# Query scores of pairs 8 to 31: turned on TensorE, or in blocks on VectorE and through DRAM

## The chip, the core and the metric

One core of a Trainium2 chip. The metric is the device time of one execution of the program, in microseconds. One core runs everything; its engines are TensorE (PE: matmuls, with PEld for the loading of weights), VectorE (DVE), ScalarE (ACT), GpSimd (POOL) and SyncE (SP), which here issues most of the DMAs.

## What is computed

A linear attention with exponential features, followed by a mixer block; batch 8, 8 heads, 576 tokens, head dimension 64, 128 features:

```
def phi(x):
    proj = einsum('bhsd,df->bhsf', x, w_phi)
    proj = proj - max(abs(proj), axis=-1, keepdims=True)
    return concatenate([exp(proj), exp(-proj)], axis=-1)
q_p, k_p = phi(q), phi(k)
kv = einsum('bhsf,bhsd->bhfd', k_p, v);  z = sum(k_p, axis=2)
x = einsum('bhsf,bhfd->bhsd', q_p, kv) / (einsum('bhsf,bhf->bhs', q_p, z) + 1e-06)
# x as [batch, 576, 512]:
u = x + (relu(x.T @ w_tok1) @ w_tok2).T        # token mix, 576 -> 256 -> 576
out = u + relu(u @ w_ch1) @ w_ch2              # channel mix, 512 -> 1536 -> 512
```

## The kernel before, in words

**Work.** Heads are taken in 32 pairs (four pairs to a batch); a pair's 2 x 64 rows fill the 128 partitions. From pair 8 on (`ROWS` = `PLAIN` = 8) an operand of a matmul is split into a high and a low part and the product is summed from three matmuls (`mm3`, line 84); pairs 0 to 7 use plain float32 matmuls and another order of the numerators (`row_numerators`, `flip`).

**Streams.** Five generators write the program: `keys()` (line 280), `queries()` (347), `token_stream()`, `load_weights()` and `channel_stream()`. `weave` (635) advances them in turns by the costs that they yield, over a share for each. A scheduler then orders the instructions of each engine with a simulated timeline; once all weights are loaded, the instructions of keys and queries have a higher priority than the rest. On the chip every engine runs its instructions in that fixed order, and a semaphore wait holds up what stands behind it.

**Keys.** For each pair `less_max` (218) projects a group of tokens (PE, `ppk`), adds the two halves of the product (`partk`, ACT, line 246; `pk`, DVE, 248), takes the largest absolute value (`mxk`, 253) and subtracts it (`pmk`, POOL, 255); ScalarE takes the exponentials `kp` (299) and PE accumulates `pkv` (324), which is copied to `kv` (341, 343). `kv` has one buffer, so a pair's `kv` is written when the numerators of the pair before are done.

**Queries.** Each pair has four pieces (k, j): k is the half of the tokens (320 or 256 of them), j the head. One step of `queries()` does, in this order: the numerators of the piece before last, the turn of the last piece, the scores of the next. Scores are `less_max` with tokens on partitions and features along them (`pmq`; the 64 last tokens of both heads are a tile of their own, `pmt`). `turn` (388 to 409) brings features to the partitions: PE transposes of 128x128 against an identity into PSUM (`pt`, line 393), three of them for k = 0 and two for k = 1, then four exponentials on ScalarE (`qf`, line 400, and rounded to float32r `qh`, 406, each with both signs), and the low parts `ql` (407, DVE and POOL). `qf`, `qh` and `ql` have two buffers each. `numerators` (463) runs `mm3` into `pn`, ScalarE copies to `xt` (478), VectorE turns the denominators in blocks (479, 484), and POOL multiplies `xt` (486).

**Buffers of a batch.** `xt0` (tokens of k = 0) has two buffers and `xt1` three: a batch's attention, its token mix (500) and the channel mix (549) of its tokens all work in them, and the channel mix's result is stored to `out_x` from there (607, 608). The channel mix goes in 18 chunks of 256 tokens (a batch has 2.25), each 6 times up (`h`) and down (`acc`). A chunk waits until the batches of its tokens are mixed, and a batch's `xt0` is free again when the chunks over its tokens are stored. PSUM: `pt`, `pn`, `ppq`, `ppt`, and from batch 1 on `pa`, `ph` and `px` share three banks (`REST`, line 56).

**Rows of batches 0 and 1.** `row_numerators` writes `rows` (438), five units of 128 tokens for a pair of pairs, two buffers; `flip` and the token mix (506) read it.

**SP's queue.** In one line: `raw` (266, one buffer, a pair's queries and the next pair's keys), `v` (290, 292), weights (139), `out_x` (608).

Of the kernel before, what the change touches and what calls it, by code (L numbers as in the profile page):

```python
# [32 lines left out]
LAST = 15  # L33
LAG = 0.02
SCRATCH = 1024
CH = 256

SEG = [(0, 320), (320, 256)]
# [7 lines left out]
def mixer_kernel(ctx, tc, qk, vm, vt, w_phi, w1, w2, wc1, wc2d, out):  # L46
    nc = tc.nc

    cst = ctx.enter_context(tc.tile_pool(name="cst", bufs=1))
    wk = ctx.enter_context(tc.tile_pool(name="wk", bufs=2))  # L50
    ps_w = ctx.enter_context(tc.tile_pool(name="ps_w", bufs=1, space=PSUM))
    ps_k = ctx.enter_context(tc.tile_pool(name="ps_k", bufs=1, space=PSUM))
    ps_h = ctx.enter_context(tc.tile_pool(name="ps_h", bufs=1, space=PSUM))
# [4 lines left out]
    def streamed(pool, shape, dtype, **kw):  # L58

        n = 1  # L60
        for k in shape[1:]:
            n *= k
        t = pool.tile([P, n + 32], dtype, **kw)[:, 16:16 + n]
        if len(shape) == 3:
            t = t.rearrange("p (a b) -> p a b", a=shape[1])
        return t
# [278 lines left out]
        kvs[i] = both  # L345

    def queries():
        turned, split_up, row_major = None, None, None
        pieces = [(i, k, j) for i in range(B * NP) for k in range(2) for j in range(2)] + [None] * 3
        for piece in pieces:  # L350
            if row_major:
                flip(*row_major)
                yield 0.2
            row_major = None
            if split_up:
                yield from until(lambda: split_up[0] in kvs)
                if split_up[0] < ROWS:
                    row_major = row_numerators(*split_up)
                else:
                    numerators(*split_up)  # L360
                yield 0.75
            split_up = None
            if turned:
                split_up = turn(*turned)
                yield 0.25
            turned = None
            if piece:
                i, k, j = piece
                if (k, j) == (0, 0):
                    plain = 0 if i < PLAIN else None  # L370
                    if i < PLAIN:
                        yield from until(lambda: i in pairs)
                        ts = pairs[i]
                    else:
                        yield from until(lambda: i + 1 in raws or i + 1 == B * NP)
                        if i + 1 == B * NP:
                            load(i + 1)
                        ts = stack(raws[i + 1], 0, f"q{i}")
                    asked.add(i)
                    tail = less_max(ts, [None], f"t{i}", plain, i < NP)  # L380
                    yield 0.11
                pm = less_max(ts, [(j, 2 * k), (j, 2 * k + 1)], f"q{i}_{k}{j}", plain, i < NP)
                turned = (i, k, j, pm, tail)
                yield 0.22

    def turn(i, k, j, pm, tail):
        w = SEG[k][1]
        ptr = ps_w.tile([P, 3, P], F32, **REST, name=f"pt{i}_{k}{j}")
        rows = [pm[:, 0], pm[:, 1]]
        if k == 0:  # L390
            rows.insert(2 * (1 - j), tail[:, 0])
        for n, r in enumerate(rows):
            nc.tensor.transpose(ptr[:, n], r, ident)  # L393

        o = D if k == 0 and j == 1 else 0
        src = ptr.rearrange("p u s -> p (u s)")[:, o:o + w]
        qps = []
        for sg in range(2):
            full = wk.tile([P, SEG[0][1]], F32, tag="qf", name=f"qf{i}_{k}{j}{sg}")[:, :w]
            nc.scalar.activation(full, src, AF.Exp, scale=1.0 - 2.0 * sg)  # L400
            if i < ROWS:
                qps.append(full)
                continue
            hi = streamed(wk, [P, SEG[0][1]], F32R, tag="qh", name=f"qh{i}_{k}{j}{sg}")[:, :w]
            lo = streamed(wk, [P, SEG[0][1]], F32R, tag="ql", name=f"ql{i}_{k}{j}{sg}")[:, :w]
            nc.scalar.activation(hi, src, AF.Exp, scale=1.0 - 2.0 * sg)  # L406
            (nc.gpsimd if sg else nc.vector).tensor_tensor(lo, full, hi.bitcast(F32), op=ALU.subtract)  # L407
            qps.append((hi, lo))
        return i, k, j, qps
# [8 lines left out]
    def row_numerators(i, k, j, qps):  # L418

        b, p = divmod(i, NP)
        h, p = divmod(p, 2)
        n = 3 - k
        if j == 0:
            sums[0] = ps_w.tile([P, 2, 3, D + 1], F32, **REST, name=f"pr{i}_{k}")
        pn = sums[0]
        at = (D if j == 1 else 0) if k == 0 else 0
        for u in range(n):
            w, c = (P, at + u * P) if u < 2 else (D, 0 if j == 1 else 2 * P)  # L430
            for sg in range(2):
                nc.tensor.matmul(pn[:w, j, u], qps[sg][:, c:c + w], kvs[i][:, sg, j],  # L432
                                 start=j == 0 and u == 0 and sg == 0, stop=j == 1 and u == n - 1 and sg == 1,
                                 skip_group_check=True)
        if j == 0:
            return None
        if (b, h) not in rows_of:
            rows_of[b, h] = wk.tile([P, 5, 2 * P], F32, tag="rows", name=f"rows{b}_{h}")
        x = rows_of[b, h][:, 3 * k:3 * k + n, p * P:p * P + P].rearrange("p u (j d) -> p j u d", j=2)
        den = column(wk, 8, tag="dn", name=f"dn{i}_{k}", bufs=4)  # L440
        if i < NP:
            gates.append(den[:, :1])
        for w, a, e in ((P, 0, 2), (D, 2, 3))[:2 - k]:
            d = den[:w, 2 * a:2 * e].rearrange("p (j u) -> p j u", j=2)
            nc.vector.tensor_scalar(d, pn[:w, :, a:e, D], 1e-6, None, op0=ALU.add)
            nc.vector.reciprocal(d, d)
            nc.vector.tensor_tensor(x[:w, :, a:e], pn[:w, :, a:e, :D],
                                    d.unsqueeze(3).to_broadcast([w, 2, e - a, D]), op=ALU.mult)
        return i, k

    def flip(i, k):
        b, p = divmod(i, NP)
        make_xts(b)
        x = rows_of[b, p // 2][:, 3 * k:3 * k + 3 - k, (p % 2) * P:(p % 2) * P + P]
        pf = ps_w.tile([P, SEG[0][1]], F32, **REST, name=f"pf{i}_{k}")[:, :SEG[k][1]]
        for u in range(3 - k):
            w = P if u < 2 else D
            nc.tensor.transpose(pf[:, u * P:u * P + w], x[:w, u], ident[:w, :w])
        nc.scalar.copy(xts[b][k][:, p], pf)
        if k == 1:  # L460
            attended.add(i)
# [28 lines left out]
    def until(cond):  # L490
        while not cond():
            yield None
# [7 lines left out]
    def token_mix(b, h, xt):  # L500
        pa = bank(b, [P, NT, 256], f"pa{b}_{h}", 0)
        for u, (s0, w, _) in enumerate(UNITS):
            k = 0 if s0 < SEG[1][0] else 1
            o = s0 - SEG[k][0]
            if (b, h) in rows_of:
                px = rows_of[b, h][:, u].rearrange("p (c d) -> p c d", c=2)
            else:
                px = bank(b, [P, 2, P], f"px{b}_{h}_{u}", 1)
                for c in range(2):
                    nc.tensor.transpose(px[:w, c], xt[k][:, 2 * h + c, o:o + w], ident)  # L510
            if w < P:

                xs = streamed(wk, [P, 2, P], F32R, tag="xh", name=f"xs{b}_{h}")
                nc.scalar.copy(xs[:w], px[:w])
                nc.vector.tensor_tensor(xs[w:], px[:w], xs[:w].bitcast(F32), op=ALU.subtract)  # L515
                x_all = xs.rearrange("p c d -> p (c d)")
                for t in range(NT):
                    ts = slice(t * P, (t + 1) * P)
                    for w1 in (w1_h, w1_l):
                        nc.tensor.matmul(pa[:, t], w1[:, u, ts], x_all, start=False, stop=False,  # L520
                                         skip_group_check=True)
                yield 0.6
                continue
            xh = streamed(wk, [P, 2, P], F32R, tag="xh", name=f"xh{b}_{h}_{u}")[:w]
            xl = streamed(wk, [P, 2, P], F32R, tag="xl", name=f"xl{b}_{h}_{u}")[:w]
            split(xh, xl, px[:w], nc.scalar, nc.gpsimd if (b, h) in rows_of else nc.vector)
            for t in range(NT):
                ts = slice(t * P, (t + 1) * P)
                mm3(pa[:, t], (w1_h[:w, u, ts], w1_l[:w, u, ts]),
                    (xh.rearrange("p c d -> p (c d)"), xl.rearrange("p c d -> p (c d)")),  # L530
                    u == 0 and t == 0, u == 4, group_ok=True)
            yield 0.8
# [165 lines left out]
```

## Time and profile before

| | |
|---|---|
| three runs | 1129.95, 1130.73, 1130.96 us; median 1130.73 |
| the profiled execution | 1130.58 us; its span, first to last instruction, 1128.8 us |
| granted TensorE clock | 0.999 of 2.4 GHz |
| PE, DVE, ACT, POOL busy | 98%, 59%, 48%, 45% of the span |
| instructions | 24388 |
| DMA | 54.39 MB in 66164 packets |

How to read it: a matmul's duration runs from its start to a modelled end, and matmuls overlap, so the sum of durations is more than the time that PE gives to them, and the distance of their ends is what one costs in a full stream. In the waits, "A <- B" is engine A standing idle until B's result came. The chain follows the end of the run back, at each step to what released the instruction. A piece's place in time can be told by its `qf` (ScalarE) and `xt` (GpSimd, line 486) instructions, a chunk's end by line 607.

### The profile page before, as it was taken

The page shows a single profiled execution, that of the slowest core. Times are in us where ns is not written, and L with a number is a line of the kernel's source. Part 1 is how long each engine was busy: PE and PEld are TensorE (multiplying, and loading weights), DVE is VectorE, ACT ScalarE, POOL GpSimd, SP SyncE. Part 2 cuts the span into 40 slices and gives each one's busy share as a digit, 9 for nine tenths or more (in the row PEclk, how much of TensorE's full clock was granted, in tenths as well). Part 3 has the DMA queues.
Part 4 walks back from the last instruction along what each step waited for, and adds up shares of the span by engine and source line. Part 5 has one row for each costly group of instructions (what it writes and reads, how often), then busy time and mean ns, then how long its engine had stood idle before and what let it go on. Part 6 is the DMA issues. An engine that isn't in the chain of part 4 may idle for free.

```text
span 1128.8 us, 24388 instructions
## 1 busy us (share of the span) xinstructions
PE 1109.2 (98%) x9280; PEld 1092.9 (97%) x9280; DVE 669.1 (59%) x1655; ACT 542.7 (48%) x1589; POOL 512.0 (45%) x675
## 2 busy tenths in 40 slices
PE   8999999999999999999999999999999999999998
PEld 7998999989999999989999999999999999999998
DVE  7889864476575756677465573664756675542111
ACT  5766543445464644556454463544645565441110
POOL 2334332465464744756364472644645474330110
PEclk9999999999999999999999999999999999999999
DMA  7545401111110111111011110111101110000000
GB/s 210 169 127 163 138 16 43 32 52 33 29 54 20 33 33 51 33 51 33 20 33 51 33 51 1 52 33 38 46 19 33 51 33 12 20 1 19 20 20 20
DMA packets 66164, 54.39 MB, mean 48 GB/s; under 512 B 44992, under 2 KB 56768, under 8 KB 66048
## 3 DMA queue, kind: packets, MB, share of 16 engines
q1 hardware_dynamic: 64528, 52.41, 15.9%
q8 instruction: 74, 1.21, 0.4%
q10 hardware_dynamic: 1520, 0.43, 0.2%
q14 instruction: 42, 0.34, 0.1%
HBM read 43.38 MB, written 9.44 MB: 47 GB/s over the span
## 4 chain that ended last, share of the span: by engine, by line
PE 87%; DVE 5%; POOL 3%; ACT 2%; DMA 2%; issue 1%; SPq 0%; POOLq 0%; ACTq 0%; DVEq 0%
PE acc L84 26%; PE h L84 26%; PE pkv L324 9%; PE pn L84 6%; PE ph L84 3%; PE pa L84 3%; PE pt L393 3%; PE pr L432 2%; PE ppk L239 2%; PE ppq L239 2%; PE px L510 1%; POOL stq L214 1%; PE ppq L243 1%; PE ppk L243 1%; DMA raw<-in_w 1%
## 5 line engine op out<-in xcount | busy, mean ns | idle before, releaser
L84 PE MATMUL acc<-gh,wc 128*128 128x256 f32 x1728 | 342.6, 283 | 0.2 <-ACT gh L576 0.2
L84 PEld LDWEIGHTS acc<-gh,wc 128*128 128x128 f32 x1728 | 275.6, 188 | 0.8 <-ACT gh L576 0.7
L84 PE MATMUL h<-uh,wc_h 128*128 128x256 f32 x864 | 245.5, 285 | 0.6 <-DVE gl L577 0.5
L84 PE MATMUL h<-uh,wc_l 128*128 128x256 f32 x864 | 244.4, 283 | 0.0
L84 PE MATMUL h<-ul,wc_h 128*128 128x256 f32 x864 | 243.6, 282 | 0.8 <-POOL ul L557 0.8
L84 PE MATMUL acc<-gl,wc 128*128 128x256 f32 x864 | 241.9, 282 | 0.0
L84 PEld LDWEIGHTS h<-uh,wc_h 128*128 128x128 f32 x864 | 162.5, 188 | 2.0 <-DVE gl L577 1.6
L84 PEld LDWEIGHTS h<-ul,wc_h 128*128 128x128 f32 x864 | 162.8, 188 | 1.2 <-POOL ul L557 1.1
L84 PEld LDWEIGHTS acc<-gl,wc 128*128 128x128 f32 x864 | 162.7, 188 | 0.0
L84 PEld LDWEIGHTS h<-uh,wc_l 128*128 128x128 f32 x864 | 162.5, 188 | 0.0
L324 PE MATMUL pkv<-v,kp 128*128 128x65 f32 (+2 forms) x1152 | 156.3, 270 | 0.6 <-ACT kv L333 0.2
L299 ACT ACTIVATE kp<-pmk 128x256 f32<-128x256 f32 (+1 forms) x320 | 109.6, 393 | 94.0 <-POOL pmk L255 76.7
L577 DVE SCALAR_TENSOR_TENSOR gl<-h,gh 128x512 fp32r<-128x512 f32 x108 | 74.4, 689 | 131.0 <-ACT gh L576 127.3
L407 POOL TENSOR_TENSOR ql<-qf,qh 128x320 fp32r<-128x320 f32 (+1 forms) x96 | 80.7, 840 | 152.7 <-ACT qh L406 146.7
L400 ACT ACTIVATE qf<-pt 128x320 f32<-128x320 f32 (+1 forms) x256 | 103.7, 417 | 94.4 <-PE pt L393 76.9
L324 PEld LDWEIGHTS pkv<-v,kp 128*128 128x128 f32 x1152 | 146.1, 191 | 2.3 <-ACT kp L299 1.2
L576 ACT ACTIVATE gh<-h 128x512 fp32r<-128x512 f32 x108 | 64.8, 600 | 131.6 <-PE h L84 130.3
L557 POOL TENSOR_TENSOR ul<-xt,uh 128x64 fp32r<-128x64 f32 (+3 forms) x120 | 60.5, 531 | 95.4 <-ACT uh L556 94.6
L84 PE MATMUL pn<-qh,kv 128*128 128x320 f32 (+1 forms) x384 | 101.0, 302 | 1.8 <-DVE xs L515 1.8
L255 POOL TENSOR_TENSOR pmk<-pk,mxk 128x256 f32<-128x256 f32 (+1 forms) x120 | 71.9, 599 | 43.7 <-DVE mxk L253 23.5
L255 POOL TENSOR_TENSOR pmq<-pq,mxq 128x256 f32<-128x256 f32 x96 | 61.6, 642 | 62.8 <-DVE mxq L253 57.6
L214 POOL TENSOR_TENSOR stq<-raw,stq 64x512 fp32r<-64x512 f32 (+1 forms) x48 | 69.7, 1452 | 37.9 <-DVE stq L213 35.3
(124 smaller groups left out, 2251.6 us busy)
## 6 DMA issues: line engine op xcount, KB each, us to landing
raw<-in_qk SPq DMA_DIRECT2D x23, 576.0 KB, 3.8
rawc<-in_wc SPq DMA_DIRECT2D x24, 512.0 KB, 4.1
v<-in_vm SPq DMA_DIRECT2D x31, 256.0 KB, 3.4
out_x<-xt SPq DMA_DIRECT2D x12, 256.0 KB, 2.2
out_x<-xt SPq DMA_DIRECT2D x16, 192.0 KB, 2.0
pair<-in_qk SPq DMA_DIRECT2D x16, 160.0 KB, 4.0
pair<-in_qk SPq DMA_DIRECT2D x16, 128.0 KB, 3.8
raw<-in_w SPq DMA_DIRECT2D x8, 256.0 KB, 5.9
```

What stands on the lines that cost most here:

```text
L84: nc.tensor.matmul(o, a, m, start=first and i == 0, stop=last and i == 2, skip_group_check=group_ok)
L214: nc.gpsimd.tensor_tensor(t[lo:lo + D], src, t[base:base + D].bitcast(F32), op=ALU.subtract)
L239: nc.tensor.matmul(ps[:, i].rearrange("p two f -> p (two f)"), t[:, c:c + P], wp2.rearrange("p two f -> p (two f)"), start=True, stop=True)
L255: eng.tensor_tensor(pm[:, :n], pr, mx[:, :n].unsqueeze(2).to_broadcast([P, n, F]), op=ALU.subtract)
L299: nc.scalar.activation(kp[:, :len(us), sg], pm[:, :len(us)], AF.Exp, scale=1.0 - 2.0 * sg)
L324: nc.tensor.matmul(o, kp[:, n, sg], v, start=g == 0 and n == 0 and sg == 0, stop=u is None, skip_group_check=True)
L393: nc.tensor.transpose(ptr[:, n], r, ident)
L400: nc.scalar.activation(full, src, AF.Exp, scale=1.0 - 2.0 * sg)
L407: (nc.gpsimd if sg else nc.vector).tensor_tensor(lo, full, hi.bitcast(F32), op=ALU.subtract)
L557: nc.gpsimd.tensor_tensor(l[:, d:d + n], t[:, c, o:o + n], h[:, d:d + n].bitcast(F32), op=ALU.subtract)
L576: nc.scalar.activation(gh, ph, AF.Relu)
L577: nc.vector.scalar_tensor_tensor(gl, ph, 0.0, gh.bitcast(F32), op0=ALU.max, op1=ALU.subtract)
```

## The change

From pair 8 on `turn` no longer transposes on PE. In the step of its scores, `across` (new) turns `pm` in 32x32 blocks on VectorE into `tq`; when both heads of a half are there, one DMA writes `tq` to a DRAM buffer and four DMAs, one for each block of 32 features, read it back as `qt`, so that the blocks come to their places; the inner run of the reads is 32 floats. The exponentials read `qt` in SBUF. The turn of a piece comes three steps later than before (`BEHIND` = 3), and before each exponential a one-column POOL copy from the latest scores into the exponential's own output makes it wait for these. At the end of the stream (no scores left) up to two pieces are turned at a step, without such copies. `tq` and `qt` use the buffers of `rows`, which becomes two tiles (three units and two), two buffers each. `TURNED` = 4 takes all four pairs of a batch.

```
+BEHIND = 3
+TURNED = 4
...
+    dram = ctx.enter_context(tc.tile_pool(name="dram", bufs=4, space=bass.MemoryType.DRAM))
...
     def queries():
-        turned, split_up, row_major = None, None, None
-        pieces = [(i, k, j) for i in range(B * NP) for k in range(2) for j in range(2)] + [None] * 3
-        for piece in pieces:
+        waiting, split_up, row_major, pm = [], [], [], None
+        pieces = [(i, k, j) for i in range(B * NP) for k in range(2) for j in range(2)]
+        n = 0
+        while n < len(pieces) or waiting or split_up or row_major:
...
+            for work in split_up:
+                yield from until(lambda: work[0] in kvs)
...
+                    numerators(*work)
                 yield 0.75
+            split_up = []
+            while waiting and len(split_up) < 2 and (waiting[0][0] <= n or n >= len(pieces)):
+                due, work = waiting.pop(0)
+                split_up.append(turn(*work, pm if via(work[0]) and n < len(pieces) else None))
+                yield 0.02 if via(work[0]) else 0.25
...
                 pm = less_max(ts, [(j, 2 * k), (j, 2 * k + 1)], f"q{i}_{k}{j}", plain, i < NP)
-                turned = (i, k, j, pm, tail)
+                if via(i):
+                    across(i, k, j, pm, tail)
+                waiting.append((n + 1 + BEHIND * via(i), (i, k, j, pm, tail)))
                 yield 0.22
+            n += 1
+    halves = {}
+    def via(i):
+        return i >= ROWS and i % NP < TURNED
+    def across(i, k, j, pm, tail):
+        n = 5 - k
+        if j == 0:
+            halves[0] = wk.tile([P, n, F], F32, tag=f"rows{k}", name=f"tq{i}_{k}")
+        t = halves[0]
+        at = 0 if j == 0 else n - 2
+        nc.vector.transpose(t[:, at:at + 2], pm)
+        if j == 0:
+            if k == 0:
+                nc.vector.transpose(t[:, 2], tail[:, 0])
+            return
+        d = dram.tile([P, n * F], F32, tag=f"half{k}", name=f"dq{i}_{k}")
+        nc.sync.dma_start(d, t.rearrange("p u f -> p (u f)"))
+        full = wk.tile([P, n, F], F32, tag=f"rows{k}", name=f"qt{i}_{k}")
+        d = d.rearrange("(a i) (u b s) -> b i u a s", a=4, b=4, s=32)
+        for b in range(4):
+            nc.sync.dma_start(full[32 * b:32 * b + 32].rearrange("p u (a s) -> p u a s", a=4), d[b])
+        halves[i, k] = full.rearrange("p u s -> p (u s)")
-    def turn(i, k, j, pm, tail):
+    def turn(i, k, j, pm, tail, behind):
         w = SEG[k][1]
-        ptr = ps_w.tile([P, 3, P], F32, **REST, name=f"pt{i}_{k}{j}")
...
+        if via(i):
+            src = halves[i, k][:, j * w:j * w + w]
+        else:
...
+            if behind is not None:
+                nc.gpsimd.tensor_copy(full[:, :1], behind[:, 0, :1])
             nc.scalar.activation(full, src, AF.Exp, scale=1.0 - 2.0 * sg)
...
+            if behind is not None:
+                nc.gpsimd.tensor_copy(hi[:, :1], behind[:, 0, :1])
             nc.scalar.activation(hi, src, AF.Exp, scale=1.0 - 2.0 * sg)
...
-            rows_of[b, h] = wk.tile([P, 5, 2 * P], F32, tag="rows", name=f"rows{b}_{h}")
+            rows_of[b, h] = [wk.tile([P, 3 - c, 2 * P], F32, tag=f"rows{c}", name=f"rows{b}_{h}{c}")
+                             for c in range(2)]
```

Lines 441, 454 and 506, which index `rows`, follow the new shape.

## Rows read from the trace of the kernel before

**Rows 1.** The page, part 1: busy time and share of the span by engine.
```profile
PE 1109.2 (98%) x9280; PEld 1092.9 (97%) x9280; DVE 669.1 (59%) x1655; ACT 542.7 (48%) x1589; POOL 512.0 (45%) x675
```

**Rows 2.** Busy time by stretch: stretch, us, then per engine busy (instructions), clock, DMA, GB/s.
```profile
222.00:1012.00 790.00, 780.62 (x6545) 773.97 (x6545) 486.46 (x1197) 408.85 (x1246) 427.69 (x558) 1.00 0.12 34
```

**Rows 3.** Waits (who, for whom: us in total, times, longest); the first two from 222 to 1012.
```profile
PE pt L393 <- POOL pmq L255: 2.1, 3, 0.8
...
POOL ql L407 <- ACT qh L406: 146.7, 50, 7.0
...
DVE stk L213 <- DMA raw<-in_qk: 8.8, 3, 4.3
```

**Rows 4.** The chain that ended last, by line, from 222 to 1012.
```profile
by line: PE acc L84 27.4%; PE h L84 26.7%; PE pkv L324 10.3%; PE pn L84 8.8%; PE pa L84 3.9%; PE ph L84 3.6%; PE pt L393 3.3%; PE ppk L239 2.7%; PE ppq L239 2.6%; PE px L510 1.5%; POOL stq L214 1.3%; issue 0.8%; POOL pmq L255 0.6%; POOL ul 
```

**Rows 5.** PE's timeline at 610 us: start, length (us), line, operation, count.
```profile
610.38 0.36 PE L84 MATMUL h<-uh,wc_h 128*128 128x256 f32 x1
610.59 0.38 PE L393 MATMUL pt<-ident,pmq 128*128 128x128 f32 x2
610.80 0.27 PE L393 MATMUL pt<-ident,pmt 128*128 128x128 f32 x1
610.83 0.36 PE L84 MATMUL pa<-xl,w_h 128*128 128x256 f32 x1
```

**Rows 6.** Groups by line and shape, whole span: count | busy us, mean ns | idle before.
```profile
L299 ACT ACTIVATE kp<-pmk 128x256 f32<-128x256 f32 x256 | 93.4, 415 | 63.6 <-POOL pmk L255 47.6 <-DVE pmk L255 8.3 <-PE pkv L324 3.5
...
L393 PE MATMUL pt<-ident,pmq 128*128 128x128 f32 x256 | 53.9, 275 | 2.5 <-POOL pmq L255 2.1 <-DVE dn L446 0.3
...
L400 ACT ACTIVATE qf<-pt 128x256 f32<-128x256 f32 x128 | 48.0, 386 | 47.3 <-PE pt L393 39.5 <-PE pr L432 7.6
...
L484 DVE STREAM_TRANSPOSE den<-few 128x256 f32<-128x256 f32 x24 | 10.6, 443 | 0.6
...
L146 POOL COPY bitsc<-dn 128x1 f32<-128x1 f32 x12 | 1.9, 186 | 1.9 <-DVE dn L446 1.8
```

**Rows 7.** Queue; DMA issues (count, KB each, us to landing); SP's issue of one (ns min/median/max).
```profile
q1 hardware_dynamic: 64528, 52.41, 15.9%
...
v<-in_vm SPq DMA_DIRECT2D x31, 256.0 KB, 3.4
...
out_x<-xt SPq DMA_DIRECT2D x12, 256.0 KB, 2.2
...
v<-in_vt SPq DMA_DIRECT2D x62, 16.0 KB, 2.1
...
L292 SPq DMA_DIRECT2D v<-in_vt x62: 469/585/1194, 14.4 to 918.5; - x62
```

**Rows 8.** ScalarE's timeline at the hand-over from pair 23 to 24.
```profile
747.90 0.37 ACT L478 COPY xt<-pn 64x256 f32<-64x256 f32 x1
...
754.53 0.43 ACT L400 ACTIVATE qf<-pt 128x320 f32<-128x320 f32 x1
...
780.53 0.65 ACT L478 COPY xt<-pn 64x320 f32<-64x320 f32 x2 [0.58 <-DMA out_x<-xt]
```

**Rows 9.** Pair 8's start (one tile's instructions; first and last start), then two timelines at 350 us.
```profile
L406 ACT ACTIVATE qh<-pt x192: 372/432/499, 222.1 to 1006.1; 128x320 fp32r<-128x320 f32 x96, 128x256 fp32r<-128x256 f32 x96
...
L514 ACT CAST xs<-rows x4: 397/404/406, 54.5 to 231.1; 64x256 fp32r<-64x256 f32 x4
...
345.11 0.74 POOL L486 TENSOR_TENSOR xt<-xt,den 128x256 f32<-128x256 f32 x1 [0.24 <-DVE den L484]
...
356.85 0.76 DVE L607 TENSOR_TENSOR xt<-acc,xt 128x256 f32<-128x256 f32 x2 [1.45 <-PE acc L84]
```

**Rows 10.** The end: timelines of GpSimd and VectorE, then the chain in order of time.
```profile
1011.86 0.74 POOL L486 TENSOR_TENSOR xt<-xt,den 128x256 f32<-128x256 f32 x1 [1.09 <-DVE den L484]
...
1015.93 0.76 DVE L607 TENSOR_TENSOR xt<-acc,xt 128x384 f32<-128x384 f32 x2 [0.54 <-PE acc L84]
...
1025.06 4.23 PE h L84 x36
```

More of the change, by code (lines that the diff above doesn't have):

```diff
@@ L347, in queries @@
     def queries():
-        turned, split_up, row_major = None, None, None
-        pieces = [(i, k, j) for i in range(B * NP) for k in range(2) for j in range(2)] + [None] * 3
-        for piece in pieces:
-            if row_major:
-                flip(*row_major)
-                yield 0.2
[L354 to L358, printed above, removed]
+        waiting, split_up, row_major, pm = [], [], [], None
+        pieces = [(i, k, j) for i in range(B * NP) for k in range(2) for j in range(2)]
+        n = 0
+        while n < len(pieces) or waiting or split_up or row_major:
+            for done in row_major:
+                flip(*done)
+                yield 0.2
+            row_major = []
+            for work in split_up:
+                yield from until(lambda: work[0] in kvs)
+                if work[0] < ROWS:
+                    row_major += [done for done in (row_numerators(*work),) if done]
                 else:
-                    numerators(*split_up)
+                    numerators(*work)
                 yield 0.75
[L362 to L368, printed above, removed]
+            split_up = []
[3 more added lines that the diff above has]
+                yield 0.02 if via(work[0]) else 0.25
+            if n < len(pieces):
+                i, k, j = pieces[n]
                 if (k, j) == (0, 0):
@@ L382, in queries @@
                 pm = less_max(ts, [(j, 2 * k), (j, 2 * k + 1)], f"q{i}_{k}{j}", plain, i < NP)
-                turned = (i, k, j, pm, tail)
+                if via(i):
+                    across(i, k, j, pm, tail)
+                waiting.append((n + 1 + BEHIND * via(i), (i, k, j, pm, tail)))
                 yield 0.22
-    def turn(i, k, j, pm, tail):
-        w = SEG[k][1]
-        ptr = ps_w.tile([P, 3, P], F32, **REST, name=f"pt{i}_{k}{j}")
[L389 to L396, printed above, removed]
+            n += 1
[21 more added lines that the diff above has]
+    def turn(i, k, j, pm, tail, behind):
+        w = SEG[k][1]
+        if via(i):
+            src = halves[i, k][:, j * w:j * w + w]
+        else:
+            ptr = ps_w.tile([P, 3, P], F32, **REST, name=f"pt{i}_{k}{j}")
+            rows = [pm[:, 0], pm[:, 1]]
+            if k == 0:
+                rows.insert(2 * (1 - j), tail[:, 0])
+            for n, r in enumerate(rows):
+                nc.tensor.transpose(ptr[:, n], r, ident)
+            o = D if k == 0 and j == 1 else 0
+            src = ptr.rearrange("p u s -> p (u s)")[:, o:o + w]
         qps = []
@@ L437, in row_numerators @@
         if (b, h) not in rows_of:
-            rows_of[b, h] = wk.tile([P, 5, 2 * P], F32, tag="rows", name=f"rows{b}_{h}")
-        x = rows_of[b, h][:, 3 * k:3 * k + n, p * P:p * P + P].rearrange("p u (j d) -> p j u d", j=2)
+            rows_of[b, h] = [wk.tile([P, 3 - c, 2 * P], F32, tag=f"rows{c}", name=f"rows{b}_{h}{c}")
+                             for c in range(2)]
+        x = rows_of[b, h][k][:, :, p * P:p * P + P].rearrange("p u (j d) -> p j u d", j=2)
         den = column(wk, 8, tag="dn", name=f"dn{i}_{k}", bufs=4)
@@ L453, in flip @@
         make_xts(b)
-        x = rows_of[b, p // 2][:, 3 * k:3 * k + 3 - k, (p % 2) * P:(p % 2) * P + P]
+        x = rows_of[b, p // 2][k][:, :, (p % 2) * P:(p % 2) * P + P]
         pf = ps_w.tile([P, SEG[0][1]], F32, **REST, name=f"pf{i}_{k}")[:, :SEG[k][1]]
@@ L505, in token_mix @@
             if (b, h) in rows_of:
-                px = rows_of[b, h][:, u].rearrange("p (c d) -> p c d", c=2)
+                px = rows_of[b, h][k][:, u - 3 * k].rearrange("p (c d) -> p c d", c=2)
             else:
```

## The prediction

> **What bounds the kernel now.** I read the page's engine totals first: PE is busy 98% of the span, no other engine over 59% [rows 1]. An average can hide stages, so next the busy time by stretch: I cut the span where the first exponential of pair 8 runs (222) and where the last numerators are divided (1012). In the middle stretch, the only one that the change touches, PE is busy 780.6 of 790 us, DVE 486, ACT 409, POOL 428, DMA 12%, and the granted clock is 1.00 [rows 2]. Then the waits: PE's longest that the change touches is 2.1 us in total over the stretch, for the very transposes that go [rows 3]. Last the chain of that stretch: 3.3% of it, 26.1 us, are the transposes `pt` of line 393 [rows 4]. So PE's instruction stream sets the time, and what counts is what an instruction keeps PE from doing next, which is not its duration: these transposes last 275 ns each [rows 6], but overlap.
>
> **Term 1, PE: the transposes go.** Pairs 8 to 31 have 3+3+2+2 transposes each: 24 x 10 = 240. In the timeline a matmul `h` starts at 610.38 and lasts 0.36, so ends at 610.74; three transposes and one `pa` matmul later the end is 610.83+0.36 = 611.19 [rows 5]. Of these 0.45 us a 256-column matmul takes 0.12 (the next `pa` starts 0.12 after); 0.33 remain, 0.111 us per transpose. 240 x 0.111 = 26.6 us; the chain's 26.1 us say the same. Nothing comes onto PE: **-26.6 us**.
> By the Trainium skill (TensorE: Matmul & The Clock Gate, PE-mode transpose) a transpose takes about 390 ns in isolation and about 275 in a kernel; an estimate from 390 would be 94 us and a time of 1043. The trace agrees with the 275 as a duration and disagrees with it as a price in a full stream.
>
> **Term 2, VectorE.** Per pair four block transposes of 128x256 and one of 128x128. A 128x256 one is in the trace at 443 ns [rows 6]; the small one is shorter, and I take it as long: 24 x 5 x 0.443 = 53 us at most. DVE goes from 486 to 539 us in a stretch that shrinks to some 764: 71%. It lies beside PE's channel matmuls, price 0; if that cover were gone, 0.44 us in the chain of each piece.
>
> **Term 3, GpSimd.** Each turned piece gets four one-column copies that hold its exponentials back until the latest score is there; pair 31 is turned in the flush, without them: 23 x 4 x 4 = 368. The trace has this copy at 186 ns [rows 6]: 68 us, POOL from 428 to 496 of 764, 65%. Behind a copy stand `pm` subtractions, splits and `ql`; for them wait the key exponentials, and PE's `pkv` for those. Price 0 beside PE, but this is the least certain engine (rival 3).
>
> **Term 4, ScalarE.** The 384 exponentials read SBUF instead of PSUM. A 128x256 one lasts 386 ns from PSUM (`qf`), 415 from SBUF (`kp`) [rows 6]: +0.03 x 384 = 11 us on ACT, 55%. Price 0; PE's `pn` would wait for it.
>
> **Term 5, transfers.** Each half pair issues one write (320 or 256 KB) and four reads, on SP: 48 x 5 = 240 DMAs. The reads move 128-byte runs, 2560 in the larger half; no row shows that size. Bounds: `v<-in_vm` lands 1024 runs of 256 B in 3.4 us, `v<-in_vt` 64 in 2.1 [rows 7], so 1.3 us for 960 more, 1.35 ns each: 2560 take 2.1 + 3.5 = 5.6 us. The other end is the mean packet of the whole queue: 15.9% of 16 engines x 1128.8 us over 64528 packets is 44.5 ns on one engine, 2560/16 of them 7.1 us, plus 2.1 [rows 7]. With 0.4 for the transpose, 0.6 to issue the write and 2.2 until it lands (as `out_x` of 256 KB), the trip is 8.8 to 12.4 us; I take 8.8, `v` being nearest in kind. A step of the query stream is 790/96 = 8.2 us, three are 24.7: the trip is home in time, price 0. SP itself: five issues of about 0.58 us [rows 7] make 2.9 us, and about 2.2 of waiting for the write, per half; behind it queue the loads `raw` and `v` and the stores of outputs. A load that comes 5 us late costs little: VectorE's `stk` waited for `raw` three times in all, 8.8 us [rows 3].
>
> **Term 6, the lag.** Numerators of a piece come three steps later. Where does that meet something? `xt0` has two buffers, so a batch's numerators wait for a chunk two batches back to be stored: the numerators stand still from 747.9 to 780.5, released by an output DMA, while the next pair's first exponentials (754.5) are long done [rows 8]. There the lag is free, for scores can run further ahead. It is not free in two places. At pair 8 no lead exists yet: its first exponential ran at 222.1, the rows buffers, which it now shares with batch 1 (the split of that tile in two costs nothing else), are read from until 231.1 [rows 9], and three steps put it up to 24.7 us later, once; chunk 3 ends at 356.9, 12 us after batch 2's numerators (345.1) [rows 9], about what the token mix needs. At the end the last trip (8.8) delays batch 7: its numerators end at 1011.9, chunk 14 at 1015.9, and the channel matmuls run unbroken from 1025 [rows 10]. Together 0 to 34 us. PE has in both places the work of pieces scored ahead, and [rows 8] is the nearest case (lag absorbed), so I take a fifth: **+6 us**. A gain is possible too: the three PSUM banks lose a user, and of the 9.4 us that PE idles in the stretch [rows 2] some may close: down to -6.
>
> **Sum.** The profiled execution took 1130.6 us (span 1128.8, 1.8 around it), the median of the three runs is 1130.7: no difference worth carrying. 1130.6 - 26.6 + 6 = **1110**; with -6 to +16 in place of +6, 1098 to 1120.
>
> **Rivals.**
> 1. *Attention, not PE, sets the pace.* Against: PE's 98.8% in the stretch. For: at batches 2 and 7 chunk and attention meet within 12 and 4 us [rows 9, 10], and the same lines show it at 3 and 6, four of the six, so a PE that is faster may only reach the hand-over earlier and wait. Then only two batches' share is kept, 26.6 x 2/6 = 8.9, and the end pays the trip of 8.8: 1130.6 - 8.9 + 8.8 = 1130.5, between 1122 and 1133.
> 2. *The trip outlasts three steps.* Then each of 48 halves is late by the excess; the gain is gone at 26.6/48 = 0.55 us of excess, a trip of 25.3 us. At 27 us it is 48 x 2.3 = 110 us: 1214. Against: 8.8 to 12.4 from the rows. It would take packets at about three times the dearer of the two prices, so the chance is small.
> The Trainium skill (DMA: Bandwidth & Descriptors, Specifications) asks for transfers of at least 512 B for line rate and has read-modify-write below that; by it the reads would come out nearer to this rival. No row of this trace shows runs of 128 B.
> 3. *Slower: GpSimd becomes what PE waits for.* POOL runs in order; two to four copies (0.37 to 0.74 us) stand ahead of a `pm` subtraction, and each waits for a `qf` or `qh` buffer that the matmuls of the piece before must free, so POOL now idles where ACT did. It decides from 26.6/92 = 0.29 us per piece that reaches PE. With 0.37: 92 x 0.37 = 34, and the lag's 6: 1144; with 0.74, 1178. For: POOL gains the most instructions (368 on 558 in the stretch [rows 2]), and already waits 146.7 us for `qh` [rows 3]. Against: PE's own waits for POOL in the stretch are the 2.1 us that go [rows 3].
> The Trainium skill (VectorE: DVE Perf Modes, Rules for kernel authors) says to turn a 128x128 tile on TensorE if PSUM will do; by it the change is a loss, as in rival 3. The trace, with PE full and DVE at 62% of the stretch, is against it.
>
> **How the numbers follow.** Forecast 0.70, rival 1 0.13, rival 2 0.05, rival 3 0.12. A measurement of this kernel tells about 0.2% from no change, 2.3 us: faster means under 1128.4. All of the forecast's case and half of rival 1 (0.06) lie there: 0.76. Rival 1 within 0.2%: 0.05. Rival 1's rest with rivals 2 and 3: 0.19. The range 1098 to 1136 reaches over rival 1 and leaves out rival 2 (0.05), most of rival 3 (0.10) and a little below.
>
> **What would show it.** Right: `pt` is left with 80 transposes (pairs 0 to 7); 120 VectorE transposes of about 0.44 us; 368 POOL copies of about 0.19; reads landing in 3 to 8 us; the stretch between pair 8's first numerators and the last about 20 us shorter at a PE busy share of still 98%; the end after the last numerators near 117 us as now. Wrong: PE idle of over 25 us in the stretch, with releasers `kp` or `pm` behind POOL copies (rival 3), `qf` behind a DMA (rival 2), or `uh`, `xh` at the hand-overs between attention and channel (rival 1). If the last numerators come no earlier than 1012, rival 1 was right.

## The result: 1137.5 us, slower by 0.6%

The median of four runs is 1137.51 us (1135.19 to 1140.06) against 1130.67: a ratio of 1.0058, 95% interval 1.0046 to 1.0070. The forecast was 1110 and the range ended at 1136; the change goes the other way.

### The profile page after: what moved, and what is told of

Same layout as the page of the kernel before. It is cut to its first block, busy times and chain, and to the rows that moved or that the text cites. A ratio compares the mean times of both kernels' runs of the same rounds, so it can differ in the third digit from the quotient of the medians.

```text
span 1134.9 us, 24670 instructions
## 1 busy us (share of the span) xinstructions
PE 1102.7 (97%) x9040; PEld 1082.1 (95%) x9040; DVE 717.6 (63%) x1775; ACT 565.7 (50%) x1589; POOL 568.2 (50%) x1043
## 4 chain that ended last, share of the span: by engine, by line
PE 77%; DVE 8%; POOL 6%; DMA 3%; ACT 3%; issue 2%; SPq 0%; ACTq 0%; POOLq 0%; DVEq 0%
PE h L87 23%; PE acc L87 23%; PE pkv L327 9%; PE pn L87 5%; PE ph L87 4%; PE pa L87 3%; PE pr L472 2%; DMA raw<-in_qk 2%; PE ppk L242 2%; PE ppq L242 1%; POOL stq L217 1%; PE px L551 1%; POOL stk L217 1%; PE ppk L246 1%; POOL pmq L258 1%
## 5 line engine op out<-in xcount | busy, mean ns | idle before, releaser
L87 PE MATMUL acc<-gh,wc 128*128 128x256 f32 x1728 | 337.1, 282 | 1.6 <-ACT gh L617 1.4
L327 PE MATMUL pkv<-v,kp 128*128 128x65 f32 (+2 forms) x1152 | 160.5, 274 | 5.4 <-DVE kv L346 4.7
L327 PEld LDWEIGHTS pkv<-v,kp 128*128 128x128 f32 x1152 | 151.5, 197 | 7.0 <-DVE kv L346 5.7
L87 PE MATMUL pn<-qh,kv 128*128 128x320 f32 (+1 forms) x384 | 105.8, 303 | 1.9 <-ACT qh L446 1.8
L438 ACT ACTIVATE qf<-qt 128x320 f32<-128x320 f32 (+1 forms) x192 | 83.3, 440 | 45.9 <-POOL qf L437 44.3
L446 ACT ACTIVATE qh<-qt 128x320 fp32r<-128x320 f32 (+1 forms) x192 | 83.5, 438 | 32.8 <-POOL qh L445 26.4
L217 POOL TENSOR_TENSOR stk<-raw,stk 64x512 fp32r<-64x512 f32 (+1 forms) x48 | 68.4, 1426 | 40.2 <-DVE stk L216 30.9
```

The lines of the kernel that those rows point to most:

```text
L87: nc.tensor.matmul(o, a, m, start=first and i == 0, stop=last and i == 2, skip_group_check=group_ok)
L217: nc.gpsimd.tensor_tensor(t[lo:lo + D], src, t[base:base + D].bitcast(F32), op=ALU.subtract)
L327: nc.tensor.matmul(o, kp[:, n, sg], v, start=g == 0 and n == 0 and sg == 0, stop=u is None, skip_group_check=True)
```

## The profile after

The page of the changed kernel, engines, slices and the DMA queue:

```profile
PE 1102.7 (97%) x9040; PEld 1082.1 (95%) x9040; DVE 717.6 (63%) x1775; ACT 565.7 (50%) x1589; POOL 568.2 (50%) x1043
...
PEclk9999999989997999999999899999999999999999
...
q1 hardware_dynamic: 185104, 80.74, 27.6%
```

The 240 transposes are gone (9280 to 9040 [rows 1]), yet PE's busy time fell by 6.5 us only, and its time outside busy grew from 19.6 us (span 1128.8 less 1109.2 [rows 1]) to 32.2 (1134.9 less 1102.7). The line of the granted clock, full in every slice before, has dips. The middle stretch, as in [rows 2]:

```profile
222.00:1012.00 790.00, 766.91 (x6236) 755.30 (x6236) 532.04 (x1307) 430.74 (x1240) 479.87 (x920) 0.98 0.28 70
```

So the profiled run (1136.7 us, 6.1 more than before's) is two losses against one gain: -26.6 for the transposes as forecast, +12.6 outside busy, and an estimate of +18.2 for the mean clock (0.999 less 0.983, times 1134.9 us); together +4.2.

**Single parts** came out as priced. Groups by line and shape, and the landing of the DMAs:

```profile
L407 DVE STREAM_TRANSPOSE tq<-pmq 128x256 f32<-128x256 f32 x96 | 42.0, 437 | 10.8 <-POOL pmq L258 10.0
L410 DVE STREAM_TRANSPOSE tq<-pmt 128x128 f32<-128x128 f32 x24 | 7.3, 305 | 3.3 <-POOL pmt L258 3.1
L445 POOL CAST qh<-pmq 128x1 fp32r<-128x1 f32 x184 | 36.7, 202 | 17.0 <-PE pn L87 15.1
L438 ACT ACTIVATE qf<-qt 128x256 f32<-128x256 f32 x96 | 38.8, 412 | 17.5 <-POOL qf L437 16.5 <-DMA qt<-dq 0.4
```

```profile
raw<-in_qk SPq DMA_DIRECT2D x23, 576.0 KB, 4.5
...
dq<-tq SPq DMA_DIRECT2D x24, 320.0 KB, 2.1
qt<-dq SPq DMA_DIRECT2D x96, 80.0 KB, 2.9
```

**Waits** that are new or longer (whole span; us, times, longest):

```profile
ACT kp L302 <- PE pkv L327: 70.0, 73, 4.4
...
ACT qf L438 <- POOL qf L437: 44.3, 63, 2.4
...
DVE stk L216 <- DMA raw<-in_qk: 25.5, 11, 4.1
...
PE pkv L327 <- DVE kv L346: 4.7, 2, 3.1
```

The key exponentials waited 3.5 us for `pkv` before [rows 6]. `kv` has one buffer and is written when the numerators of the pair before are done, so later numerators can hold up the keys. `raw` was 8.8 us in three waits [rows 3].

**Where the time goes.** Windows round the hand-over of batch 2 to chunk 4 (stretch, us, busy of PE, PEld, DVE, ACT, POOL, clock, DMA share, GB/s), then timelines in it:

```profile
340.00:350.00 10.00, 10.00 (x88) 10.00 (x87) 7.28 (x19) 6.29 (x20) 8.38 (x19) 1.00 0.28 69
350.00:360.00 10.00, 6.47 (x34) 4.72 (x33) 9.37 (x26) 5.56 (x17) 8.96 (x16) 0.86 0.48 120
360.00:370.00 10.00, 7.85 (x33) 6.45 (x31) 5.39 (x14) 4.17 (x11) 5.32 (x9) 0.50 0.44 114
```

```profile
350.29 0.76 DVE L648 TENSOR_TENSOR xt<-acc,xt 128x256 f32<-128x256 f32 x2 [0.27 <-PE acc L87]
...
365.32 0.41 PE L87 MATMUL pa<-xh,w_h 128*128 128x256 f32 x1
365.54 0.41 PE L87 MATMUL pa<-xl,w_h 128*128 128x256 f32 x1
...
369.68 0.71 POOL L527 TENSOR_TENSOR xt<-xt,den 128x256 f32<-128x256 f32 x1
...
381.63 0.28 PE L87 MATMUL ph<-w_h,ah 128*128 128x256 f32 x1
381.75 0.28 PE L87 MATMUL ph<-w_l,ah 128*128 128x256 f32 x1
```

Batch 2's last numerators come at 369.7 instead of 345.1 [rows 9]: 24.6 us, three steps, as the prediction had it. Chunk 3 ends at 350.3, 6.6 us earlier than before. The order is turned over: before, attention was done 12 us ahead of the chunk; now the channel mix has nothing to do for the 19 us until batch 2 is there. PE idles 3.5 of the ten us from 350, in gaps of 1.43 us at most; the clock falls to 0.50 (1.2 of 2.4 GHz), and 256-column matmuls start 0.22 us apart instead of 0.12.

The next such place is at 620 us:

```profile
617.78 0.62 SPq L269 DMA_DIRECT2D raw<-in_qk  x1
...
622.45 0.42 DVE L216 CAST stk<-raw 64x512 fp32r<-64x512 f32 x1 [2.95 <-DMA raw<-in_qk]
622.90 0.76 DVE L346 TENSOR_TENSOR kv<-pkv,kv 128x256 fp32r<-128x256 f32 x2
...
623.71 3.67 PE L327 MATMUL pkv<-v,kp 128*128 128x65 f32 x16 [3.09 <-DVE kv L346]
```

`raw` is issued between two reads of the trip, lands late, VectorE stands at `stk` for 2.95 us; behind `stk` in its order is the copy of `kv`, for which PE waits 3.09 us. In the stretch 620 to 630 the clock is 0.67.

## The experiments

The theories when they began, with the letters that the expectations use: the **lag** (A: late numerators starve the channel mix; later D: they also hold up `kv` and with it the keys), the **copies** (B: GpSimd, rival 3), and the **trip** (C: waiting for `qt`, or what its DMAs do to other loads). Times are medians; the ratio and its 95% interval are against the kernel before, run beside it.

### One part undone

**lag1**: `BEHIND` = 1.

```diff
-BEHIND = 3
+BEHIND = 1
```

> One number changed: the turn comes one step later than before the change, not three. Theory A (the lag of three steps delays batch 2's attention by 25 us, chunk 4 then starves, PE idles and its clock falls to half): two steps of 8.2 us less lag, so batch 2's last numerators about 16 us earlier than 369.7, the idle and half-clock time between 350 and 390 nearly gone, and 1137 - 15 = about 1122. Theory B (GpSimd's one-column copies delay pm and with it PE): as many copies, so 1133 to 1140. Theory C (SP's queue delays the loads raw): as many transfers, 1133 to 1140, or slower where the exponentials now wait for the trip.

1147.16 us, ratio 1.0146 (1.0129 to 1.0163). Batch 2 ends at 365.1, 4.6 us earlier and not 16, and the exponentials now wait for the trip:

```profile
ACT qf L438 <- DMA qt<-dq: 91.8, 40, 5.4
```

With a lag of three the same wait is 0.4 us in all. The lag does what it is for, and rival 2 falls.

**from12**: pairs 8 to 11 as before.

```diff
-        return i >= ROWS and i % NP < TURNED
+        return i >= 12 and i % NP < TURNED
```

> The change from pair 12 on; pairs 8 to 11 keep the transposes on TensorE and the old lag. Theory A: batch 2's attention ends near 345 as in the kernel before, chunk 4 starts on time, and at pair 12 the lag falls into the standstill for xt0; 200 transposes of 0.111 us go, 22 us, with the later losses of some 15 us kept: 1115 to 1125. Theory B or C: five sixths of the change's effect, so 1134 to 1137.

1137.42 us, 1.0060 (1.0045 to 1.0075): no difference, and the 1115 to 1125 of theory A is missed. Batch 2 ends at 344.7 as before, but the stall has moved one batch on (batch 3 ends at 495.3 instead of 476.9):

```profile
480.00:490.00 10.00, 6.35 (x20) 3.98 (x21) 7.70 (x21) 4.72 (x15) 9.56 (x17) 0.65 0.46 110
490.00:500.00 10.00, 8.84 (x40) 8.11 (x40) 3.94 (x11) 4.31 (x13) 4.03 (x7) 0.50 0.28 68
```

So the stall goes where the lag begins, and a lead over the channel mix did not absorb it.

**nogate**: no one-column copies.

```diff
-                split_up.append(turn(*work, pm if via(work[0]) and n < len(pieces) else None))
+                split_up.append(turn(*work, None))
```

> The change without the 368 one-column copies on GpSimd; the exponentials may go as soon as their qt has landed. Theory A: the order of the exponentials moves a little, the lag in the numerators stays, 1132 to 1140. Theory B: POOL falls from 568 to about 500 us busy, PE's idle time falls by 10 us or more, 1112 to 1125. Theory C: 1133 to 1140.

1135.55 us, 1.0040 (1.0025 to 1.0055): at best 2 us. `qf` then waits 64.1 us for `qt`, where it waited 0.4 with the copies. The keys wait far less:

```profile
ACT kp L302 <- PE pkv L327: 10.9, 12, 2.1
```

That wait falls from 70.0 us and the time hardly moves; but the wait for `qt` has come in its place, so this run prices neither.

**notrip**: no DMAs; the exponentials read `tq`, so the kernel leaves out putting the 32x32 blocks in their places; all sizes stay.

```diff
-        d = dram.tile([P, n * F], F32, tag=f"half{k}", name=f"dq{i}_{k}")
-        nc.sync.dma_start(d, t.rearrange("p u f -> p (u f)"))
...
-        halves[i, k] = full.rearrange("p u s -> p (u s)")
+        halves[i, k] = t.rearrange("p u s -> p (u s)")
```

> The change without the DRAM trip: the exponentials read the block-turned tile tq itself, so the 32 by 32 blocks stay where they are and the data is not put in place; the 240 transfers and SP's share in them are left out, VectorE's turns, the copies and the lag stay. Theory A: 1132 to 1140. Theory B: 1133 to 1140. Theory C: VectorE waits for raw 9 us as before the change instead of 25.5, PE's waits for kv behind it go, 1120 to 1130.

1124.35 us, 0.9942 (0.9927 to 0.9956). The trip costs 13 us, though in the change hardly anything waits for its end (0.4 us on ScalarE, 0.9 on GpSimd).

### Down to the floor

**notrip_lag1** is notrip with `BEHIND` = 1; **notrip_lag1_ng** also leaves the copies out; **notrip_ng** is notrip without the copies at lag 3.

> As notrip (exponentials read the block-turned tile, blocks not put in place, no transfers), and the turn comes one step later, not three. Theory D (kv has one buffer, so numerators that come three steps later hold up the keys, ScalarE's kp waits for pkv): those waits fall from 64 us in notrip to under 15, and the time from 1124 to between 1106 and 1115. If the lag has no price of its own: 1120 to 1128.

> As notrip_lag1, and without the one-column copies on GpSimd: what the change would give if the blocks came to their places at no cost. Theory B (the copies have a price): at least 5 us less than notrip_lag1. Otherwise within 3 us of it. A floor for the whole idea is 1131 - 26.6 = 1104.

> No transfers (blocks not put in place), lag of three steps, no one-column copies. If the copies make the lag (without them the scheduler lets the exponentials go early, and nothing holds the keys): 1103 to 1108, as with lag 1, and ScalarE's kp waits for pkv under 15 us. If the lag has its price without them: 1110 to 1120.

1112.31 (0.9844, 0.9827 to 0.9860), 1103.01 (0.9755, 0.9741 to 0.9770) and 1111.12 us (0.9824, 0.9810 to 0.9839). The page of notrip_lag1_ng, its wait of the keys, and the same wait in notrip_ng:

```profile
PE 1085.9 (99%) x9040; PEld 1070.1 (97%) x9040; DVE 715.9 (65%) x1775; ACT 559.0 (51%) x1589; POOL 509.8 (46%) x675
```

```profile
ACT kp L302 <- PE pkv L327: 3.5, 5, 1.4
...
ACT kp L302 <- PE pkv L327: 29.6, 36, 2.9
```

The turns, with exponentials from SBUF and a lag of one step, gain 27.7 us: terms 1, 2 and 4 together.

**idle_trip** is the other half alone: before's transposes and order of steps, with the VectorE turns and all 240 DMAs issued as work that nothing reads (`turn` always takes the PE branch, `BEHIND` out).

> The kernel before in its order of work (transposes on TensorE, no lag, no copies), with VectorE's block turns and all 240 transfers done beside it as work whose result nobody reads. Theory C (SP's queue and VectorE's load cost by themselves): 8 to 13 us more than before, 1139 to 1144, with VectorE waiting for raw some 20 us in place of 9. If they cost only where the exponentials wait for them: 1130 to 1134.

1132.97 us, 1.0017 (1.0008 to 1.0026): 2.2 us. The order on PE is not quite that of the kernel before: at 2279 of 9280 places another instruction stands.

**deadpe** keeps 240 PE transposes in the changed kernel, unread.

```diff
+                    idle = ps_w.tile([P, 3, P], F32, **REST, name=f"pd{i}_{k}{j}")
...
+                        nc.tensor.transpose(idle[:, m], r, ident)
```

> The change, and the 240 transposes on TensorE kept beside it as work whose result nobody reads (in the step of the scores). Theory A' (PE's own stream still sets the time, and the change only adds waits to it): 240 x 0.111 = 26.6 us come back, 1137 + 26.6 = 1160 to 1166. Theory D (attention with its lag sets the pace at the hand-overs, PE has time to spare there): most of the 26.6 us fit into the idle time and keep the clock up, 1137 to 1148.

1213.26 us, 1.0733 (1.0717 to 1.0749), outside both expectations. Inconclusive: the unread transposes take one of the three shared PSUM banks for a time, and wait there for `pm` (28.7 us), so it prices more than an instruction.

### What about the transfers costs 13 us

**dead_trip**: all DMAs, but the exponentials read `tq`; **dead_trip_lag1** the same with `BEHIND` = 1.

```diff
-        halves[i, k] = full.rearrange("p u s -> p (u s)")
+        halves[i, k] = t.rearrange("p u s -> p (u s)")
```

> Lag of three steps and the copies as in the change; all 240 transfers are issued and land, but the exponentials read the block-turned tile (blocks not put in place), so nobody waits for them. If the trip's 13 us come from the transfers' presence (SP's queue before raw, buffers held): 1133 to 1140, with VectorE waiting for raw over 20 us. If they come from the exponentials having to follow the trip: 1122 to 1128, notrip's 1124 plus the 2 us of idle_trip.

> The same with a lag of one step. If the 35 us between notrip_lag1 (1112) and lag1 (1147) are the exponentials' waits for the trip: 1111 to 1117. If the presence of the transfers costs as at lag 3: 1122 to 1128 or more.

1138.09 (1.0064, 1.0048 to 1.0079) and 1114.21 us (0.9848, 0.9832 to 0.9865). At lag 3 the presence of the transfers costs 13.7 us, at lag 1 only 1.9. These pairs are clean: on PE, VectorE, ScalarE and GpSimd, notrip and dead_trip hold the same instructions in the same order (4 of 9040 places differ on PE, 2 of 1775 on VectorE), and dead_trip has that of the change; at lag 1 no place differs. What differs can be followed at one place. Timelines of notrip, then of dead_trip, the same instructions:

```profile
358.24 1.53 POOL L217 TENSOR_TENSOR stk<-raw,stk 64x640 fp32r<-64x640 f32 x1
...
359.80 0.35 SPq L269 DMA_DIRECT2D raw<-in_qk  x1
...
363.29 0.42 DVE L216 CAST stk<-raw 64x512 fp32r<-64x512 f32 x1 [0.38 <-DMA raw<-in_qk]
```

```profile
361.30 1.53 POOL L217 TENSOR_TENSOR stk<-raw,stk 64x640 fp32r<-64x640 f32 x1
...
363.75 0.58 SPq L269 DMA_DIRECT2D raw<-in_qk  x1
364.38 2.35 SPq L417 DMA_DIRECT2D qt<-dq  x3
...
368.59 0.42 DVE L216 CAST stk<-raw 64x512 fp32r<-64x512 f32 x1 [2.63 <-DMA raw<-in_qk]
369.05 0.76 DVE L346 TENSOR_TENSOR kv<-pkv,kv 128x256 fp32r<-128x256 f32 x2
...
369.86 1.41 PE L327 MATMUL pkv<-v,kp 128*128 128x65 f32 x6 [2.50 <-DVE kv L346]
```

The buffer of `raw` is free when `stk` ends. Without transfers the load is issued 0.03 us later and lands in 3.5 us; with them 0.92 us later, behind a read, and it lands in 4.8. That is 2.2 us, which stand as 2.63 us of VectorE and then, because the copy of `kv` is queued behind, as 2.50 us of PE. Windows of two us, notrip and then dead_trip:

```profile
368.00:370.00 2.00, 2.00 (x19) 2.00 (x19) 0.55 (x2) 1.25 (x6) 0.00 (x1) 1.00 0.00 0
370.00:372.00 2.00, 2.00 (x18) 2.00 (x17) 1.60 (x6) 1.15 (x4) 0.49 (x2) 1.00 0.57 130
```

```profile
366.00:368.00 2.00, 1.35 (x8) 1.07 (x7) 0.00 (x0) 1.26 (x4) 0.00 (x0) 0.84 1.04 272
368.00:370.00 2.00, 0.14 (x1) 0.14 (x2) 1.35 (x4) 0.00 (x0) 0.85 (x1) 1.00 0.13 20
370.00:372.00 2.00, 2.00 (x11) 2.00 (x11) 1.52 (x5) 0.27 (x1) 1.92 (x3) 0.51 0.00 0
...
378.00:380.00 2.00, 2.00 (x10) 2.00 (x11) 0.48 (x2) 0.87 (x3) 0.00 (x0) 0.50 0.03 8
```

In notrip the clock is back at 1.00 from 364 on. In dead_trip it had just come back when PE was empty for nearly two us, and the next ten run at 0.50, with 11 matmuls in two us instead of 18. The sums say that this is nearly all: from notrip to dead_trip PE's busy time grows by 13.8 us for the same 9040 instructions, its time outside busy by 1.2.

As the order is one, each PE instruction of dead_trip can be set against the same one of notrip. By notrip's time it starts 0.3 us earlier at 223, 2.7 later at 243, 3.1 at 354, 10.1 at 375, still 10.1 at 597, 14.5 at 627 and 15.0 at the end. So three places make nearly all of it: 11 us fall where `raw` is late (the one above and one like that at 620), but the first 3 us do not. There the gaps of PE before the two rows below are as long in both (the longest 1.36 us), none of them for `raw`, and only the clock comes back later; why, no run shows. First notrip, then dead_trip:

```profile
238.00:240.00 2.00, 2.00 (x17) 2.00 (x17) 1.03 (x4) 0.78 (x3) 1.88 (x2) 1.00 0.00 0
```

```profile
238.00:240.00 2.00, 2.00 (x11) 2.00 (x11) 0.39 (x2) 0.34 (x2) 1.90 (x2) 0.50 0.60 95
```

The cells side by side (profiled runs; "outside" is span less PE busy):

| lag, copies, transfers | median us | PE busy | outside | clock |
|---|---|---|---|---|
| before | 1130.7 | 1109.2 | 19.6 | 0.999 |
| 1, no, none | 1103.0 | 1085.9 | 15.4 | 0.998 |
| 1, yes, none | 1112.3 | 1085.7 | 23.8 | 1.000 |
| 1, yes, unread | 1114.2 | 1088.5 | 24.2 | 0.998 |
| 3, no, none | 1111.1 | 1089.7 | 20.6 | 0.993 |
| 3, yes, none | 1124.4 | 1092.0 | 29.6 | 0.992 |
| 3, yes, unread | 1138.1 | 1105.8 | 30.8 | 0.978 |
| 3, yes, read (the change) | 1137.5 | 1102.7 | 32.2 | 0.983 |
| 3, no, read (nogate) | 1135.6 | 1100.2 | 34.4 | 0.989 |

Against the floor (the second row) the change has lost 33.6 us of span: 16.8 in PE's busy time for as many instructions, about what the lower clock accounts for (0.998 less 0.983, times 1134.9 us, is 17.0), and 16.8 outside it. What one part costs hangs on the others: without the copies the transfers cost 24.4 us at lag 3 (notrip_ng to nogate), with them 34.9 at lag 1 (notrip_lag1 to lag1), since in both the exponentials wait for `qt`.

### Other queues, lags and buffers

**raw_act** and **raw_pool** issue `raw` on ScalarE's and GpSimd's queue instead of SP's:

```diff
-                nc.sync.dma_start(raw[lo:hi], qk[i, lo:hi])
+                nc.gpsimd.dma_start(raw[lo:hi], qk[i, lo:hi])
```

> The change, with the 25 loads raw issued on ScalarE's queue, so that they no longer stand behind the trip's writes and reads on SP. Theory C (the trip's 13 us come from raw behind SP's queue): VectorE's waits for raw fall from 25.5 to about 10 us, the time from 1137 to 1124 to 1128. If the trip's price lies elsewhere (the order of work that the longer way of the scores gives): 1133 to 1140.

> The same with the loads raw on GpSimd's queue, which itself frees the buffer that they fill. Theory C: 1124 to 1130. Otherwise 1133 to 1142, as GpSimd also pays for issuing them.

1142.18 (1.0087, 1.0062 to 1.0112) and 1128.96 us (0.9978, 0.9961 to 0.9996); `stk` waits 14.2 and 17.0 us for `raw`, both less than 25.5. The control is **before_rawpool**, the kernel before with the same edit:

> Control: the kernel before, with the loads raw on GpSimd's queue. If raw_pool's 8 us came from the trip standing before raw in SP's queue: no gain here, 1129 to 1134. If those loads wait on SP in any case: 1121 to 1126.

1137.72 us, 1.0058 (1.0043 to 1.0073), with a clock of 0.998. The edit lets the scheduler write another order: at 2547 of 9280 places PE runs another instruction. `stk` also waits longer for `raw`, 17.3 us where it was 8.8 [rows 3], so queue and order are not told apart here. Either way the edit moves this kernel by 7 us where there is no trip to get out of the way of, and the +4.7 and -8.5 us of the two queues can't be put down to the trip standing before `raw`.

**lag2_ng** (`BEHIND` = 2, no copies), **rawpool_ng** (raw_pool, no copies) and **rawpool_lag2_ng** (both) look for a better point:

> The change with a lag of two steps and without the one-column copies: the lag and the copies cost less, the trip more, as exponentials may wait for it. If the two prices balance as between lag 1 (1147) and lag 3 (1137): 1134 to 1142. If the keys' hold-up weighs most: 1128 to 1133.

> The change with raw on GpSimd's queue and without the one-column copies. If the prices of SP's queue and of the copies add up: 1129 - 2 to 1129 - 9, so 1120 to 1127, faster than both kernels. If the exponentials then wait for the trip (64 us in nogate): 1127 to 1133.

> The same with a lag of two steps. If the exposed trip sets the time (lag2_ng 1143 against nogate 1136): 1130 to 1138. If the lag does: 1115 to 1125.

1143.47 (1.0111, 1.0096 to 1.0126), 1142.13 (1.0097, 1.0065 to 1.0130) and 1127.34 us (0.9968, 0.9951 to 0.9985). The last computes all of the reference and is faster than both kernels, by 0.3%, though its single runs lie between 1123 and 1132. raw_pool without its copies is 13 us slower; its exponentials then wait 51.4 us for `qt`, and `stk` 30.5 for `raw`. All three missed their expectations, so the parts did not add up as thought, and how much of that is the order's is not shown.

**psum2** gives `pkv` two PSUM banks and the shared users two instead of three:

> The change, with two PSUM banks for pkv and two instead of three shared by the rest (the transposes pt no longer use them from pair 8 on). Theory D (numerators three steps later hold the single kv, with it pkv and the keys): ScalarE's waits of kp for pkv fall from 70 to under 25 us, 1137 - 12 = about 1125, less what the lost bank costs. If the lag's price is another one: 1135 or more.

1215.18 us, 1.0745 (1.0729 to 1.0761), but the wait that the second bank was to end is gone, from 70.0 us:

```profile
ACT kp L302 <- PE pkv L327: 1.3, 2, 0.9
```

So the third shared bank is worth more than what `pkv` could gain, and the gain can't be read from this run. A second buffer for `kv`, with all banks left, was not tried.

## Why the prediction was wrong, step by step

- **Term 1** (-26.6) held: -27.7 down to the floor, and 23.3 of that in PE's busy time (1109.2 to 1085.9). The floor has another order than the kernel before, so a match within 1 us is closer than this can be known. The 0.12 us that it takes for a matmul is the distance of two ends, not of two starts as it says: the `pa` after the one at 610.83 starts at 611.03 and ends at 611.31, 0.12 after.
- **Terms 2 and 4** (price 0) held: 437 and 305 ns for a turn, 412 for an exponential from SBUF, and the floor, which holds both, is 1 us below what term 1 alone gives.
- **Term 6** (+6) failed: "[rows 8] is the nearest case (lag absorbed), so I take a fifth". The delay of 24.6 us and its place were right. But with the delay attention is 19 us behind the chunk there, and from12 shows that the lag is not absorbed where it begins later either. Without transfers two more steps of it cost 8.1 us without copies and 12.0 with them (1103.0 to 1111.1, 1112.3 to 1124.4). The step left out that PE, faster now, finishes chunk 3 earlier (350.3) while attention comes later, and that `kv` is held longer: without copies and transfers `kp` waits for `pkv` 29.6 us at lag 3 where it waits 3.5 at lag 1. Which of the two makes the price is not shown.
- **Term 3** (0) failed in its price, not in its duration (202 ns against 186). Without transfers the copies cost 9.3 us (lag 1) and 13.2 (lag 3), in the change 2.0. Copies and lag each come with another order (48 to 58% of PE's 9040 places differ), so these sizes hold whatever the order alone moves, which no run prices. Rival 3's 34 us and more is not there: no wait of PE for POOL is over 1.6 us in total.
- **Term 5** was right on the trip itself. In the change a write is issued at 349.64, and its four reads between 352.42 and 355.10; the last lands at 357.6. That is 8.0 us, with the turn's 0.4 8.4, against the 8.8 that was taken. It failed at "a load that comes 5 us late costs little", which took the three waits of [rows 3] as the price. What is queued behind `stk` on VectorE was not named: the copy of `kv`, and PE's `pkv` behind that. Price at lag 3: 13.7 us, shown by the pair in one order, of which the places with a late `raw` make 11 of 15 us in the profiled runs; at lag 1, where the clock stays at 0.998, 1.9.
- **The clock** is in no term. With 1.00 in the stretch before [rows 2] I took it as given; in the change PE idles 3.5 of ten us from 350 and 3.09 us in one gap at 620, the rows there show 0.50 and 0.67, and about half of what was lost against the floor is this. The Trainium skill (TensorE: Matmul & The Clock Gate, HAM oscillation — how this bites in real kernels) describes a kernel whose clock falls again at each wait of its matmuls for a DMA; the window from 368 in dead_trip, with 0.51 in the next, agrees.
- **The sum.** By one way up the table: 1103.01, lag +8.11, copies +13.23, transfers +13.74, reading what they bring -0.58: 1137.51. Another way gives other shares, as the cells show. Three costs that I had looked at one by one and each set at nothing or nearly so, because [rows 2] showed room on every engine.
- **Rivals.** The first came nearest: its sign, "the last numerators come no earlier than 1012", is met (1015.3), and the place is the hand-over between attention and channel. The other sign is not: PE idles 23.1 us in the stretch, under the 25 named, and its longest waits are for `kv` (4.7) and `gl` (4.1), not for `uh` or `xh`. Its price was too low, as it let PE wait at full clock and charged nothing for the load of `raw`. The second is refuted (0.4 us of waiting in all). The Trainium skill (DMA: Bandwidth & Descriptors, Specifications) asks for 512 B or more; the reads of 128-byte runs landed in 2.9 us, so the rule decided nothing here. The third is told under term 3.

Not settled: how much of the 8 to 13 us of lag and copies belongs to them and how much to the order that comes with them, why the clock came back later at 238 in dead_trip, and what a second buffer of `kv` would give back.

## What to carry to other kernels

Before a step is moved later, write down at every hand-over which side is ahead and by how much; where the lead is less than the delay, the consumer starves. When a DMA is put ahead of another in a queue, follow the waiting instruction to what stands behind it on its engine, down to the bottleneck. A gap of the busiest engine costs more than its length when the clock falls after it, so count gaps of TensorE at the clock that the rows show behind them, and where a scheduler writes the order, price an edit only against a pair with the same order or a control.

## What the runs showed that was not expected

- Two programs with one order and nearly equal idle time of PE (29.6 and 30.8 us) differ by 13.7 us, nearly all of it in PE's busy time, at a granted clock of 0.992 and 0.978.
- The nine runs of raw_act, one program, lie between 1132.8 us at a clock of 0.992 and 1145.8 at 0.976: once PE has gaps, its time is spread as well as longer. The kernel before, at 0.998 to 1.000, stayed within 1130.0 and 1133.3 beside it.
- An edit without a gain of its own, another queue for one load, slowed the kernel before by 0.58%, with another order and longer waits for that load; which of them did it is not shown.
- Reads of 64 and 80 KB in runs of 128 bytes land in 2.8 to 2.9 us, while SP takes 0.63 us to issue one (its median for line 417) and 0.34 for the write of 256 or 320 KB. Here they cost by what stands behind them in the queue.
